# A causal retention layer with a gated unit behind it: the second double chunk's queries in a gate bank, its scores ahead of the first's values, the w_out load between two casts, and three double chunks with load buffers of their own

## The chip, the cores and the metric

The kernel runs on one NeuronCore of a Trainium2 chip. Its metric is the time on the device of one execution, in microseconds (us), as the median of repeated runs. TensorE is called PE here (PEld is its loading of weights), VectorE DVE, ScalarE ACT, GpSimd POOL, and SyncE, which issues most of the transfers, SP.

## The reference

Eight sequences of 576 tokens, 8 heads of 64 values each. The first half is retention: attention without a softmax, whose scores are causal and fall off with the distance by a factor gamma per head. The second is a gated unit: the retention's output, with the heads side by side (512 values per token), goes through a causal convolution of 5 taps per column and a sigmoid to make a gate, and through a matrix to make the value; the product goes through a second matrix.

```python
scores = scale * np.matmul(q, k.transpose(0, 1, 3, 2))      # per batch and head
gamma = 1.0 - 2.0 ** (-5.0 - np.arange(H))
Dmat = np.where(rel >= 0, gamma ** rel, 0.0)                # rel = query's place - key's place
x = np.matmul(scores * Dmat, v)                             # heads side by side: (B, S, 512)
for k in range(5):
    gate_pre += conv_w[k] * xp[:, k:k + S, :]               # xp: x with 4 zero rows ahead
gate = 1.0 / (1.0 + np.exp(-gate_pre))
out = (gate * (x @ w_val)) @ w_out
```

Inputs and output are float32; the kernel multiplies in bf16.

## The kernel before

The work is cut into 18 "double chunks", numbered from 0 in the list `dcs`. A sequence gives two full double chunks of 256 tokens; the last 64 tokens of four sequences together make a tail. The order is sequences 0 to 3 with two double chunks each, their tail (number 8), then sequences 4 to 7 and their tail (17). So double chunks 0 and 1 are the two of sequence 0, 2 and 3 those of sequence 1.

Gamma to the power of the distance is split into two factors: values are multiplied by `gin` when they are cast to bf16, and the result by `gout`. So a mask of zeros and ones is all that the scores need, and what earlier double chunks contribute is a state, keys times values, that is carried on.

For a double chunk m these are the steps, with the helper that issues each:

- `load` (through `fetch`, L87) issues three transfers of 512 KB on SP: keys, queries, values, into tiles `fk`, `fq`, `fv` of the pool `ld`. Double chunks 0 and 1 use tiles of the names `fke`, `fqe`, `fve`; all others share two buffers of each of `fk`, `fq`, `fv`, so the load of m+2 waits for the cast of m.
- `cast_k`, `cast_q` (L224) and `cast_v` (L240) turn them into bf16 on POOL: about 1.04, 1.04 and 1.90 us.
- `turn(0, m)` and `turn(1, m)` (L262) transpose keys and queries, 8 TensorE transposes each, into a PSUM bank: by default the only bank of the pool `ps_t` (`tps`), or one that is given. `take_turned` (L270) copies the bank into the tile `kq`, by default on ScalarE (1.02 us).
- `scores(m, r)` are 16 matmuls (L252, s<-kq) for each of the two halves r of the keys, into the banks s0 and s1 of `ps_s`. `masks` (L293) multiplies each bank by the mask on VectorE (0.69 us) into the tiles p0 and p1 of the pool `pp`, which has two buffers of each.
- `values` (L307, o<-p,vb) are 16 matmuls per r; `carried` (L307, o<-kq,sd) adds the state's part. `take_x` (L342) multiplies the two result banks by `gout` on VectorE into the long tile `x`. `pass_on` (L355) copies the last four columns of `x` to the next double chunk's tile on POOL; the convolution needs them.
- `update` (L252, st<-vb,kb) adds to the state, `take_state` (L377) copies it to bf16 on ScalarE.
- `conv` (L252, g<-x,dg) is the convolution as 40 matmuls with diagonal matrices; `gate` (L406) the sigmoid on ScalarE; `value` (L413) the matmuls with w_val in bf16 (`wvb`) and a product with the gate on VectorE (L416, tile z); `project` (L423) the matmuls with w_out (`wob`), a copy on ScalarE (L431) and the store. All of these use the pool `ps_g`, two PSUM banks of the name g: the gate banks.

The order on each engine is the program's: the body is written under a manual schedule, so engines run their instructions in the order of the text, and only waits between engines are added.

A prologue (L451 to L500) does double chunk 0 without its convolution, together with the constants. Dummy matmuls on a tile of zeros (`keep_warm`, L448) fill TensorE's waits. Then a loop runs m from 1 to 18. Pass m does the scores, values and state of double chunk m, and the convolution and gate of m-1; the values with w_val and the projections follow behind (in passes 2 and 3 those of the first two double chunks catch up). Pass m also turns keys and queries of m+1, casts m+2 and issues the loads of m+4.

Weights: w_val comes in three transfers, two on SP behind the loads of double chunk 2 (L109, L110) and one on ACT (L113). It is cast in two halves, `prep_wv(g_copy, 1)` on POOL at the end of the prologue and `prep_wv(s_copy, 0)` on ScalarE in pass 2 (L215). w_out comes in three transfers that POOL issues (L124, L126), which convert it to bf16 on the way.

Of the kernel before, what the change touches and what calls it, by code (L numbers as in the profile page):

```python
# [13 lines left out]
F32 = mybir.dt.float32  # L14
BF16 = mybir.dt.bfloat16
# [6 lines left out]
def kernel(  # L22
# [57 lines left out]
    with tc.manual_schedule():  # L80
# [12 lines left out]
                                      in_=src[GB * b + 2 * r + ab, :, c * W:S, :].rearrange("h p d -> p h d"))  # L93

        def load(name, m):
            t = ld.tile([P, H, R, D], F32, name=f"f{name}" + ("e" if m < 2 else ""))
            fetch(nc.sync, t, {"q": q, "k": k, "v": v}[name], m)
            loaded[name, m] = t

# [12 lines left out]
        def load_wv_rest():  # L112
            nc.scalar.dma_start(out=wv_dst[1, half[1]], in_=wv_src[1, 0])  # L113

        for name in "kqv":
            load(name, 3)


        ORDER = ((0, 0, 0, 1), (HP, 0, 1, 0), (0, 2, 0, 0), (HP, 2, 1, 1))
# [109 lines left out]
        def cast_k(m, *copies):  # L229
            cast("k", m, copies)  # L230

        def cast_q(m, *copies):
            cast("q", m, copies)
# [22 lines left out]
        def turn(which, m, bank=None):  # L256

            src = (kbf, qbf)[which][m]
            dst = new_bank() if bank is None else bank
            for pr in range(NP):  # L260
                for r in range(R):
                    nc.tensor.transpose(dst[:, pr, r, :], src[:, pr, r, :, :].rearrange("p i d -> p (i d)"), ident)  # L262
            return dst

        def take_turned(which, m, bank, *copies):
            if m not in kq:
                kq[m] = tp_sb.tile([P, 2, NP, R, P], BF16, name="kq", bufs=2)
            o = 0
            for (copy, n) in copies or ((nc.scalar.copy, NP),):
                copy(kq[m][:, which, o:o + n], bank[:, o:o + n])  # L270
                o += n
            assert o == NP
# [65 lines left out]
        def take_x(m, ab):  # L338
            kind, b, c = dcs[m]
            if kind == "full":  # L340
                t0, x0 = c * W + ab * P, PAD + ab * P
                nc.vector.tensor_tensor(  # L342
                    xg[b // GB][c][:, b % GB, :, x0:x0 + P].rearrange("p o (n r) -> p o r n", r=R),
                    ops[m, ab], gout[:, :, t0:t0 + P].rearrange("p o (r n) -> p o r n", r=R), op=ALU.mult)
            else:
                nc.vector.tensor_tensor(
                    xg[b][c][:, ab::2, :, PAD:].rearrange("p b o n -> p o b n"),
                    ops[m, ab], gout[:, :, c * W:S].unsqueeze(2).to_broadcast([P, NP, R, TAIL]), op=ALU.mult)

        def pass_on(m):  # L350

            kind, b, c = dcs[m]
            if kind == "full":
                x = xg[b // GB]
                nc.gpsimd.tensor_copy(x[c + 1][:, b % GB, :, 0:PAD], x[c][:, b % GB, :, W:W + PAD])  # L355
# [87 lines left out]
        def keep_warm(n, t=None):  # L443

            if t is None:
                t = ps_o.tile([P, NP, R, HP], F32, name="o0").rearrange("p o r n -> p (o r n)")
            for _ in range(n):
                nc.tensor.matmul(t, zeros[:, 0:P], zeros, start=True, stop=True)  # L448
# [28 lines left out]
        run(update(0, 0))  # L477
        take_state(0, 0)
        load_wv_rest()
        keep_warm(1)  # L480
        run(update(0, 1))
        take_state(0, 1)
        run(carried(0, 1))
        bank = turn(0, 1)
        take_turned(0, 1, bank)
        keep_warm(2, spare(ps_g, "g"))
        bank = turn(1, 1)
        take_turned(1, 1, bank)
        run(*values(0, 1))
        run(*values(0, 0))  # L490
        run(carried(0, 0))
        take_x(0, 0)
        take_x(0, 1)
        pass_on(0)
        keep_warm(4, spare(ps_g, "g"))
        for (name, f) in (("k", cast_k), ("q", cast_q), ("v", cast_v)):
            f(2)
            load(name, LB + 2)
        prep_wv(g_copy, 1)
        load_wo()  # L500

# [1 line left out]
        for m in range(1, ND + 1):  # L505
            now, nxt, last = ok(m), ok(m + 1), m == ND
            late = m < 4
            hi, lo = conv(m - 1)

            if now:  # L510
                run(scores(m, 0))
                masks(m, 0, 0)
                masks(m, 0, 1)
            if last:
                run(lo, hi)
                gate(m - 1, 1)
                gate(m - 1, 0)
            elif late:
                run(lo[0:8], hi[0:8])
                run(pairs(update(m, 0)), hi[8:10])  # L520
                take_state(m, 0)
                gate(m - 1, 0)
                run(pairs(update(m, 1)), lo[8:10])
                take_state(m, 1)
                gate(m - 1, 1)
                run(carried(m, 1))
            else:
                run(carried(m, 1))
                run(pairs(update(m, 1)), lo[0:2])
                take_state(m, 1)  # L530
                run(lo[2:10], hi[0:8])
                gate(m - 1, 1)
                run(pairs(update(m + 1, 0)), hi[8:10])
                take_state(m + 1, 0)
                gate(m - 1, 0)
            if now:
                run(scores(m, 1))
                masks(m, 1, 0)
                masks(m, 1, 1)

            if last:
                value(m - 1, 1, spare(ps_s, "s1"))
                value(m - 1, 0, spare(ps_s, "s0"))
                project(m - 2, 0)
                project(m - 2, 1)
                project(m - 1, 0, last=True)
                project(m - 1, 1, last=True)
                continue
            if nxt:
                bank = turn(0, m + 1)  # L550
                take_turned(0, m + 1, bank)

            if m == 2:
                prep_wv(s_copy, 0)
            for (f, n, i) in {1: (), 2: ((value, 0, 1), (value, 0, 0)),
                              3: ((value, 2, 1), (project, 0, 0), (project, 0, 1))}.get(
                                  m, ((value, m - 1, 1), (project, m - 2, 0))):
                f(n, i)
            if ok(m + 2):
                cast_k(m + 2)  # L560
                cast_q(m + 2)
                cast_v(m + 2)

            run(*values(m, 1))
            run(*values(m, 0))
            run(carried(m, 0))
            take_x(m, 0)
            take_x(m, 1)
            pass_on(m)

            if nxt:
                bank = turn(1, m + 1)
                take_turned(1, m + 1, bank)
            for (f, n, i) in {1: (), 2: ((value, 1, 1), (value, 1, 0)),
                              3: ((value, 2, 0), (project, 1, 0), (project, 1, 1))}.get(
                                  m, ((value, m - 1, 0), (project, m - 2, 1))):
                f(n, i)
            for name in "kqv":
                if ok(m + 2 + LB):
                    load(name, m + 2 + LB)  # L580
            if m == 3:
                run(update(m + 1, 0))
                take_state(m + 1, 0)
# [28 lines left out]
```

## Time and profile before

| | |
|---|---|
| median of 13 runs | 168.21 us (165.92 to 172.5) |
| the profiled execution | 168.04 us |
| its span in the profile | 166.2 us |
| around the span | 1.84 us |
| busy: PE, PEld, DVE, ACT, POOL | 88%, 65%, 60%, 55%, 48% of the span |
| moved by DMA | 39.82 MB, 240 GB/s over the span |
| start of pass 3 on TensorE | 35.52 us |

The span runs from the first to the last instruction that the hardware profiler saw. A line of a timeline gives the start, the length, the engine, the source line, the operation, output and input tiles, and in brackets the time that the engine stood idle just before and what ended it. "issue" there means that nothing which the profile shows was waited for. The clock is the share of TensorE's full clock that was granted.

### The profile page before, as it was taken

How to read it: one execution, taken by the hardware profiler on the slowest of the kernel's cores; microseconds unless marked ns; L12 is line 12 of the kernel's file. 1: busy time of each engine (PE TensorE's matmuls, PEld its weight loads, DVE VectorE, ACT ScalarE, POOL GpSimd, SP SyncE). 2: the span in 40 equal slices, each digit the busy share in tenths (PEclk: the TensorE clock that was granted, in tenths of full speed). 3: DMA queues.
4: the chain of work that ended last, by engine and by line, in shares of the span. 5: the costliest groups of instructions: out<-in, count | busy, mean ns of one | idle time of the engine just before them, and what ended most of it. 6: DMA issues, size and time to landing. Idle time of an engine off the chain costs nothing.

```text
span 166.2 us, 7603 instructions
## 1 busy us (share of the span) xinstructions
PE 146.4 (88%) x3350; PEld 107.2 (65%) x3383; DVE 100.4 (60%) x187; ACT 91.8 (55%) x149; POOL 80.0 (48%) x88
## 2 busy tenths in 40 slices
PE   6887638898999999999999997999699999999970
PEld 2455527575676867777677866686568778765620
DVE  6775461495447667666577765776567668666210
ACT  4774624426666657664667656575557575652340
POOL 4796569714883633457745734463727224000000
PEclk9999985799999999999999999999999999999997
DMA  4999999977999977999999698959994874131134
GB/s 141 345 347 309 310 265 241 273 171 197 293 373 310 302 174 182 289 332 324 347 335 296 226 297 234 325 184 311 307 312 133 190 180 181 37 130 65 66 126 126
DMA packets 70814, 39.82 MB, mean 240 GB/s; under 512 B 15978, under 2 KB 65662, under 8 KB 70782
## 3 DMA queue, kind: packets, MB, share of 16 engines
q1 hardware_dynamic: 68096, 38.28, 77.8%
q0 software_dynamic: 2352, 0.53, 2.6%
q10 hardware_dynamic: 334, 0.53, 1.2%
q8 instruction: 26, 0.43, 1.0%
q14 instruction: 6, 0.05, 0.1%
HBM read 30.42 MB, written 9.44 MB: 240 GB/s over the span
## 4 chain that ended last, share of the span: by engine, by line
PE 68%; DMA 15%; SPq 7%; issue 4%; ACT 2%; POOL 2%; DVE 1%; ACTq 0%
PE g L423 17%; PE g L413 15%; PE g L252 11%; DMA wob<-in_moe_w_out_dram 9%; PE tps L262 9%; PE o L307 7%; SPq L87 7%; DMA wvf<-in_moe_w_val_dram 6%; PE s L252 5%; PE st L252 2%; PE s L413 1%; ACT ob L431 1%; POOL wvb L215 1%; POOL wob L124 1%; DVE ob L429 1%
## 5 line engine op out<-in xcount | busy, mean ns | idle before, releaser
L293 DVE TENSOR_TENSOR p<-s,mask 128x512 bf16<-128x512 f32 x62 | 40.0, 686 | 23.1 <-PE s L252 23.0
L270 ACT COPY kq<-tps 128x1024 bf16<-128x1024 bf16 x34 | 34.6, 1018 | 17.1 <-PE tps L262 16.9
L240 POOL TENSOR_TENSOR vb<-fv,gin 128x1024 bf16<-128x1024 f32 x16 | 30.5, 1904 | 18.0 <-DMA fv<-in_v_dram 18.0
L413 PE MATMUL g<-x,wvb 128*128 128x256 bf16 x272 | 36.0, 277 | 0.8 <-ACT wvb L215 0.5
L423 PE MATMUL g<-wob,z 128*128 128x512 bf16 x113 | 34.8, 379 | 1.8
L252 PE MATMUL g<-x,dg 64*64 64x256 bf16 x720 | 32.1, 278 | 2.2 <-issue 1.4
L431 ACT COPY ob<-g 128x512 f32<-128x512 f32 x34 | 19.9, 586 | 24.7 <-PE g L423 21.8
L342 DVE TENSOR_TENSOR x<-o,gout 128x512 bf16<-128x512 f32 x32 | 22.2, 744 | 13.9 <-PE o L307 13.9
L416 DVE TENSOR_TENSOR z<-gate,g 128x512 bf16<-128x512 f32 x34 | 23.4, 687 | 10.7 <-PE g L413 9.9
L413 PEld LDWEIGHTS <-wvb 128*128 128x128 bf16 x288 | 27.0, 99 | 4.3 <-ACT wvb L215 1.0
L406 ACT ACTIVATE gate<-g 128x512 f32<-128x512 f32 x36 | 21.3, 604 | 10.7 <-PE g L252 5.4
L252 PEld LDWEIGHTS <-dg 64*64 64x64 bf16 x720 | 23.5, 107 | 5.5 <-issue 4.4
L224 POOL CAST qb<-fq 128x1024 bf16<-128x1024 f32 x16 | 16.7, 1043 | 9.6 <-PE tps L262 4.4
L423 PEld LDWEIGHTS <-z 128*128 128x128 bf16 x144 | 14.0, 98 | 10.8 <-issue 0.6
L224 POOL CAST kb<-fk 128x1024 bf16<-128x1024 f32 x16 | 16.7, 1044 | 5.4 <-DMA fk<-in_k_dram 5.1
L252 PE MATMUL s<-kq 64*64 64x128 bf16 (+1 forms) x560 | 16.3, 220 | 2.4 <-ACT kq L270 1.3
L252 PEld LDWEIGHTS <-kq 64*64 64x64 bf16 x576 | 11.8, 108 | 9.4 <-issue 8.8
L355 POOL COPY x<-x 128x16 bf16<-128x16 bf16 x16 | 3.2, 198 | 28.2 <-DVE x L342 28.2
L252 PE MATMUL st<-vb,kb 64*64 64x64 bf16 x512 | 14.1, 196 | 1.8 <-ACT sd L377 1.2
L377 ACT CAST sd<-st 128x256 bf16<-128x256 f32 x24 | 8.9, 370 | 11.8 <-PE g L252 7.1
L252 PEld LDWEIGHTS <-kb 64*64 64x64 bf16 x512 | 12.5, 112 | 3.4 <-issue 3.2
L262 PE MATMUL tps<-ident,kb 128*128 128x128 bf16 x144 | 12.0, 230 | 2.1 <-issue 1.5
(73 smaller groups left out, 120.8 us busy)
## 6 DMA issues: line engine op xcount, KB each, us to landing
out_dram<-ob SPq DMA_DIRECT2D x32, 256.0 KB, 3.9
fk<-in_k_dram SPq DMA_DIRECT2D x14, 512.0 KB, 5.9
fq<-in_q_dram SPq DMA_DIRECT2D x14, 512.0 KB, 6.4
fv<-in_v_dram SPq DMA_DIRECT2D x14, 512.0 KB, 7.5
fke<-in_k_dram SPq DMA_DIRECT2D x2, 512.0 KB, 5.0
fqe<-in_q_dram SPq DMA_DIRECT2D x2, 512.0 KB, 5.5
fve<-in_v_dram SPq DMA_DIRECT2D x2, 512.0 KB, 6.0
fk<-in_k_dram SPq DMA_DIRECT2D x8, 128.0 KB, 3.1
```

The lines of the kernel that those rows point to most:

```text
L224: copy(t[:, o:o + n], src[:, o:o + n])
L240: eng.tensor_tensor(vbf[m][:, h:h + n], loaded["v", m][:, h:h + n], g[:, h:h + n].unsqueeze(3).to_broadcast([P, n, R, D]), op=ALU.mult)
L252: return lambda: nc.tensor.matmul(*a, skip_group_check=True, **kw)
L262: nc.tensor.transpose(dst[:, pr, r, :], src[:, pr, r, :, :].rearrange("p i d -> p (i d)"), ident)
L270: copy(kq[m][:, which, o:o + n], bank[:, o:o + n])
L293: nc.vector.tensor_tensor(p[:, :, 0:n], sps[m, r][i][:, :, 0:n], mask[dcs[m][0], r].unsqueeze(1).to_broadcast([P, NP, n]), op=ALU.mult)
L342: nc.vector.tensor_tensor(xg[b // GB][c][:, b % GB, :, x0:x0 + P].rearrange("p o (n r) -> p o r n", r=R), ops[m, ab], gout[:, :, t0:t0 + P ...
L406: nc.scalar.activation(t, gps[n][i], AF.Sigmoid)
L413: nc.tensor.matmul(vps[:, j, :], lhsT=wvb[:, o, 2 * i + j, :], rhs=xs(n, slice(0, P), o, PAD), start=(j == 0 and o == 0), stop=(j == 1 and ...
L416: nc.vector.tensor_tensor(z, gsb[n][i], vps, op=ALU.mult)
L423: nc.tensor.matmul(o, lhsT=zsb[n, j // 2][:, j % 2, i * P:(i + 1) * P], rhs=wob[:, j, :], start=(j == 0), stop=(j == NP - 1))
L431: nc.scalar.copy(ob, o)
```

## The change

Six things are different.

- Double chunk 2 also gets load buffers of its own (three buffers of `fke`, `fqe`, `fve`), so the shared ones begin with double chunk 3, and the loads of double chunk 4 are issued at the start of the program behind those of 3 instead of between the casts of 2.
- In the prologue the queries of double chunk 1 are turned into a gate bank instead of `tps`, and copied half by ScalarE, half by VectorE.
- The first scores of double chunk 1 move from pass 1 into the prologue, ahead of the values of double chunk 0. Of their two masks one stands ahead of the x products of double chunk 0, one behind them.
- Keys of double chunk 2 are turned in the prologue (they were turned in pass 1), and its queries in pass 1 where the keys were, ahead of the values instead of behind them.
- In pass 2 the keys of double chunk 3 are turned behind the values of double chunk 0 with w_val instead of ahead of them.
- POOL casts keys and queries of double chunk 2 before it hands on x of double chunk 0, then issues the loads of w_out, then casts the values of double chunk 2 and its half of w_val. The dummy matmuls are placed differently; there are seven of them from there on as before.

```diff
@@ load
-            t = ld.tile([P, H, R, D], F32, name=f"f{name}" + ("e" if m < 2 else ""))
+            t = ld.tile([P, H, R, D], F32, name=f"f{name}" + ("e" if m < 3 else ""),
+                        bufs=3 if m < 3 else LB)
...
-        for name in "kqv":
-            load(name, 3)
+        for m in range(3, 5):
+            for name in "kqv":
+                load(name, m)
@@ prologue
         load_wv_rest()
-        keep_warm(1)
         run(update(0, 1))
         take_state(0, 1)
         run(carried(0, 1))
         bank = turn(0, 1)
         take_turned(0, 1, bank)
-        keep_warm(2, spare(ps_g, "g"))
-        bank = turn(1, 1)
-        take_turned(1, 1, bank)
+        bank = turn(1, 1, spare(ps_g, "g", [P, NP, R, P], BF16))
+        take_turned(1, 1, bank, (s_copy, 2), (v_copy, 2))
+        keep_warm(4)
+        run(scores(1, 0))
+        masks(1, 0, 0)
         run(*values(0, 1))
         run(*values(0, 0))
         run(carried(0, 0))
         take_x(0, 0)
         take_x(0, 1)
+        masks(1, 0, 1)
+        cast_k(2)
+        bank = turn(0, 2)
+        take_turned(0, 2, bank)
+        cast_q(2)
         pass_on(0)
-        keep_warm(4, spare(ps_g, "g"))
-        for (name, f) in (("k", cast_k), ("q", cast_q), ("v", cast_v)):
-            f(2)
-            load(name, LB + 2)
+        load_wo()
+        cast_v(2)
         prep_wv(g_copy, 1)
-        load_wo()
+        keep_warm(3, spare(ps_g, "g"))
@@ loop
-            if now:
+            if now and m > 1:
                 run(scores(m, 0))
                 masks(m, 0, 0)
                 masks(m, 0, 1)
...
-            if nxt:
-                bank = turn(0, m + 1)
-                take_turned(0, m + 1, bank)
+            def turn_keys():
+                if nxt and m > 1:
+                    bank = turn(0, m + 1)
+                    take_turned(0, m + 1, bank)
+
+            def turn_queries():
+                if nxt:
+                    bank = turn(1, m + 1)
+                    take_turned(1, m + 1, bank)
+
+            if m > 2:
+                turn_keys()
+            if m == 1:
+                turn_queries()
 
             if m == 2:
                 prep_wv(s_copy, 0)
...
                 f(n, i)
+            if m == 2:
+                turn_keys()
...
             pass_on(m)
 
-            if nxt:
-                bank = turn(1, m + 1)
-                take_turned(1, m + 1, bank)
+            if m > 1:
+                turn_queries()
```

## The prediction

> **What bounds the kernel now.** I read the page's busy shares and its 40 slices first, then TensorE's timeline up to 45 us, its busy time in stretches of 3.41 us, and last the timelines of POOL and SP. Below, "chunk" is a double chunk, counted from 0.
>
> ```profile
> PE 146.4 (88%) x3350; PEld 107.2 (65%) x3383; DVE 100.4 (60%) x187; ACT 91.8 (55%) x149; POOL 80.0 (48%) x88
> PE   6887638898999999999999997999699999999970
> ...
> PEclk9999985799999999999999999999999999999997
> ```
>
> TensorE is the bound, with eights and nines from slice 9 on (37 us). What is not full lies in the first 33 us: idle slices, and three at 8, 5 and 7 tenths of the clock. So the start decides: whatever makes the loop reach chunk 3 earlier comes off the end, if transfers keep up.
>
> ```profile
> 13.19 0.61 PE L262 MATMUL tps<-ident,qb 128*128 128x128 bf16 x8 [0.67 <-ACT kq L270]
> ...
> 15.84 1.07 PE L252 MATMUL g<-x,dg 64*64 64x256 bf16 x32
> ...
> 22.68 0.42 PE L252 MATMUL s<-kq 64*64 64x128 bf16 x16 [1.10 <-ACT kq L270]
> 22.90 0.42 PE L252 MATMUL g<-x,dg 64*64 64x256 bf16 x8
> 24.71 1.50 PE L252 MATMUL g<-x,dg 64*64 64x256 bf16 x24 [1.40 <-issue]
> ...
> 31.56 1.05 PE L413 MATMUL g<-x,wvb 128*128 128x256 bf16 x8 [0.52 <-ACT wvb L215]
> ...
> 35.52 0.42 PE L252 MATMUL s<-kq 64*64 64x128 bf16 x16
> ```
>
> This is TensorE's timeline (start, length, last the idle time and its releaser). 15.84 and 22.90 are the gate convolutions of chunks 0 and 1, 35.52 is the first instruction of chunk 3 (loop pass m=3): my milestone. Query turns wait because keys and queries share one bank (0.67, and behind it 1.10). The 1.40 us has no releaser. Counting TensorE's instructions in program order (weight loads too), it stands at about the 705th, the 0.30 us "issue" wait at 17.42 some 256 earlier, and those at 81.70, 101.62 and 117.75 again whole multiples of 256 on, give or take ten: the sign of instructions fetched in blocks.
>
> ```profile
> 17.20:20.61 3.41, 2.19 (x82) 1.75 (x86) 1.29 (x2) 2.76 (x5) 1.69 (x2) 1.00 1.12 305
> 20.61:24.03 3.42, 1.60 (x62) 1.17 (x50) 2.28 (x4) 1.01 (x1) 1.96 (x3) 1.00 0.96 260
> 24.03:27.44 3.41, 2.29 (x63) 1.96 (x65) 0.39 (x1) 0.77 (x2) 3.41 (x5) 0.50 1.02 276
> 27.44:30.86 3.42, 3.42 (x51) 2.61 (x43) 1.29 (x2) 2.37 (x5) 3.42 (x5) 0.50 1.13 240
> ```
>
> Columns: stretch, length, busy PE, PEld, DVE, ACT, POOL (with counts), clock, DMA share, GB/s. After a stretch with TensorE 47% busy the clock is halved for 6.8 us; after 64% it was not.
>
> **The change, part by part.**
>
> *Chunk 1's queries in a gate bank, its scores early.* The query turn no longer waits for the key copy: its cast ends at 11.01+1.04 = 12.05. ScalarE copies the keys at 12.12–13.13, then its half of the queries (0.585, the 128x512 row) to 13.72; VectorE's half waits for that (as its row at 8.70 does) and adds 0.42: 14.17, against 14.84 before. But four dummy matmuls and the scores now stand ahead of chunk 0's values, which move from 13.72 to 14.4. One mask (0.65) stands ahead of the two x products on VectorE. It also waits for the r=1 values: the mask tiles have two buffers each, both full. So the mask runs 14.9–15.55, the x products (1.37) until 16.92 instead of 15.78, and the convolution starts at 16.98: **+1.14 us**. Behind the waiting mask stand just those x products, and the convolution waits for them.
>
> *Chunk 2's keys ahead of the loop, its queries in their place, no turn at the end of m=1.* The 8 transposes lie where TensorE waits for x anyway (15.4–16.0; the key cast, freed of waiting for the hand-over of x, runs 14.35–15.4). Before, convolution to end of scores took 15.84–18.82; if the block at 17.42 is now in time (it is wanted 0.84 later and came 0.30 late), scores end at 19.66. Masks 19.75–21.05, values 21.1, x at 21.86–23.23 (21.03–22.40 before). Query copy 20.3–21.3, so the 1.10 us wait goes: scores of chunk 2 at 21.8. What is late next is x: convolution of chunk 1 at 23.25, **+0.35** on 22.90.
>
> *The block and the clock.* Not to be seen in advance. If the block is there, 20.61–24.03 holds values and state products 0.75, scores 0.4, convolution 0.78: 1.93 of 3.42, 56%, between the 47% that halved the clock and the 64% that didn't. If it comes as late as before, 46%. A wait for it costs between 0 and (7.29 us from one crossing to the arrival, 17.42 to 24.71, laid on the new crossing at 18.26) 25.55−23.65 = 1.9 us. Most blocks of the steady part are run through in about 5 us without a wait, and this one would be asked for 5.3 us later; I take 0 and full clock.
>
> [...]
>
> *Chunk 3's keys behind the values of chunk 0 in m=2.* From 23.25, convolution and state updates take 2.63−0.30 = 2.33 (m=1's own rows), scores to 25.93, value 1 to 26.8. ScalarE now casts its half of w_val straight after the gates (26.55–27.7, rows 1.14) instead of behind a 1.01 us key copy; value 0 waits for it, 27.7–28.6. Key turn to 29.05, values and state products to 29.75, key copy 29.25–30.26, so the query turn waits 0.5 (one bank again), 30.3–30.75; two values (1.84 before) and m=3 starts at 32.6: **−2.9** on 35.52.
>
> *w_out earlier.* Its issue (0.92+1.63) moves on POOL from behind w_val's cast to behind the hand-over of x, about 17.1–19.7, ahead of chunk 2's value cast, which waits for its transfer till 19.73 anyway, and ahead of w_val's cast, which started at 23.09 when its last piece landed. So it costs POOL nothing, and chunk 3's key cast moves from 26.70 to 24.25. If that cover goes, values of chunk 2 are late by up to 2.5 us, of which 4.3 are spare (21.63 to their use at 25.99). Gain: the projections at 40.12 stood 0.4 us for w_out (8 matmuls in 2.11 against 8 x 0.216): **−0.4**. [...]
>
> *Own buffers.* SP issued without a break from 18.57 to 24 us, so chunk 4's loads were not waiting for buffers: nothing.
>
> *Give-back.* Chunk 5's v cast ended at 46.29 and is used at 48.39; 3.3 us earlier means 45.09. If transfers land as before, **+1.2**; if they follow the earlier casts, 0. I take 1.2.
>
> **Sum**: 168.04 (span 166.2 and 1.84 around it) − 2.9 − 0.4 + 1.2 = **165.9 us**. The profiled execution is 0.17 below the median of 168.21.
>
> **Rivals.**
>
> *Block late and half clock again (0.34).* For: the 46% above. From a restart at 24.71 to 25.55 half-clock rows give scores ending 28.35, value 1 until 30.1, value 0 until 31.0, key turn, then a query turn at 32.65 and m=3 at 34.95, each plus up to 0.84: −0.6 to +0.3, with w_out's −0.4 167.0 to 167.9. Here the parts cancel: what the bank saves goes to the later x.
>
> *w_out in the way (0.20): slower.* Its transfer now flies beside w_val and chunk 3's loads.
>
> ```profile
> 24.20 0.92 POOL L124 DMA_DIRECT2D wob<-in_moe_w_out_dram  x1
> ...
> 26.70 1.08 POOL L224 CAST kb<-fk 128x1024 bf16<-128x1024 f32 x1
> ...
> 39.58 1.90 POOL L240 TENSOR_TENSOR vb<-fv,gin 128x1024 bf16<-128x1024 f32 x1 [5.79 <-DMA fv<-in_v_dram]
> ```
>
> While it flew (24.2 to 41.0), a v transfer took 13.8 us to land, against a median of 7.5: 6.3 more. On chunk 3's keys (landed by 26.70) that means 33.0, cast 34.04, and from key turn to m=3 it is 4.0: 38.05, +2.5, less 0.4: 170.1. It decides from a landing after 30.9 on. Against: the neighbours of w_out before had slack, and 4.2 us must be lost first. [...]
>
> *The rest (0.02)*: the clock lost for more stretches, above 171.
>
> **Chances.** One per cent (1.7 us) is about what a measurement of this kernel can tell. Forecast 0.44 (164.7 with no give-back to 166.3), all faster; late block 0.34, same; w_out 0.20 and the rest 0.02, slower. Range: 164.3 (no give-back and half of the 0.9 us that chunk 2's value 0 waits) to 170.1. The forecast's own range is 164.3–166.3.
>
> **What would show it.** Right: convolution of chunk 0 about 17.0 and of chunk 1 about 23.3, without an issue wait behind its first matmuls; clock 1.0 over 24–31; m=3 near 32.6; w_out landed before the first projection; a wait for chunk 5's values near 45. Wrong: half clock again, a key cast of chunk 3 beginning after 31, or x of chunk 0 well after 17.

## The result, and the profile after

| | before | after |
|---|---|---|
| median, with the number of runs | 168.03 us (48 runs, 165.92 to 172.5) | 168.09 us (11 runs, 164.22 to 169.13) |
| mean of all these runs | 168.37 ± 0.22 us | 167.36 ± 0.49 us |
| ratio | | 0.990, 95% interval 0.985 to 0.995 |
| the profiled execution, its span | 168.04, 166.2 us | 168.8, 167.1 us |

The ratio leaves out the runs that are over 1.5% above the fastest of their kernel (in the result that leaves 4 of the changed kernel's 11), so it can say "1.0% faster" although the two plain medians agree. Because the single runs are spread over 5 to 7 us, I give the mean of all runs (± its standard error) beside every ratio below. The changed kernel was timed twice more in the experiments. The means of all three sets put it below the kernel before, by 0.9 to 1.6 us; the ratios of the two repeats are 1.0000 and 0.9986, and by themselves they show no difference. So the direction rests on the means and on the traces, and the size is less certain than the first interval suggests.

The profiled execution of the changed kernel is not its median: its span is 0.9 us longer than the one of before. What that 0.9 us is made of can be read off, and it is the main lesson of this case. First the page of the changed kernel (busy shares, TensorE's 40 slices and the granted clock in tenths; its line numbers are two higher than before).

```profile
PE 146.1 (87%) x3349; PEld 107.1 (64%) x3383; DVE 100.7 (60%) x188; ACT 91.3 (55%) x149; POOL 80.2 (48%) x88
...
PE   6888746898999999999979979999799999999970
...
PEclk9999996999999999999999999999999999999999
```

The hole in the clock is shorter (one slice at 6 tenths where there were 8, 5 and 7), and the slices before it are filled no better. TensorE's timeline (start, length, the instruction, the idle time before it and what ended it):

```profile
14.56 0.31 PE L254 MATMUL s<-kq 64*64 64x128 bf16 x8 [0.28 <-ACT kq L272]
...
17.62 1.07 PE L254 MATMUL g<-x,dg 64*64 64x256 bf16 x32 [0.53 <-DVE x L344]
...
19.03 0.30 PE L254 MATMUL g<-x,dg 64*64 64x256 bf16 x2 [0.22 <-issue]
...
22.57 0.43 PE L254 MATMUL s<-kq 64*64 64x128 bf16 x16
24.22 0.41 PE L254 MATMUL g<-x,dg 64*64 64x256 bf16 x8 [1.21 <-DVE x L344]
26.05 1.08 PE L254 MATMUL g<-x,dg 64*64 64x256 bf16 x24 [1.43 <-issue]
...
33.28 0.61 PE L264 MATMUL tps<-ident,qb 128*128 128x128 bf16 x8 [0.42 <-ACT kq L272]
...
35.57 0.42 PE L254 MATMUL s<-kq 64*64 64x128 bf16 x16
```

The 0.67 and 1.10 us waits for the key copy are gone. In their place stand 0.53 and 1.21 us for x, as the prediction said. But the wait without a releaser is back behind the same eight matmuls, and just as long: 1.43 us at 26.05 (1.40 at 24.71 before). Pass 3 starts at 35.57, not at 32.6. The stretches that held the clock show what follows from the wait (busy PE, PEld, DVE, ACT, POOL, then clock, DMA share, GB/s):

```profile
20.61:24.03 3.42, 1.78 (x67) 1.43 (x64) 2.53 (x4) 1.61 (x3) 2.81 (x4) 1.00 1.19 304
24.03:27.44 3.41, 1.80 (x52) 1.45 (x53) 1.30 (x3) 0.00 (x0) 0.97 (x1) 0.87 1.24 228
27.44:30.86 3.42, 2.92 (x57) 2.09 (x50) 1.42 (x3) 2.77 (x6) 1.04 (x1) 0.63 0.78 185
```

TensorE is 52% and 53% busy in the first two, and the clock is halved towards the end of the second. In the profiles here the half clock lasts 3.4 (result), 6.8 (before) or 10.2 us (e1), that is one, two or three steps of 3.41 us, and the stretches above are not in line with these steps. The following ones are, in the same columns: two of this profile, then one of the first repeat of the changed kernel (e0) and one of a run with dummy matmuls (f1), both described below.

```profile
23.13:26.54 3.41, 0.90 (x28) 0.63 (x32) 2.20 (x4) 0.00 (x0) 1.87 (x3) 1.00 1.27 214
26.54:29.95 3.41, 2.98 (x80) 2.40 (x69) 0.59 (x1) 2.08 (x5) 1.04 (x1) 0.50 0.87 211
...
20.05:23.46 3.41, 1.86 (x75) 1.46 (x64) 2.43 (x4) 1.70 (x3) 3.08 (x4) 1.00 1.17 311
...
23.38:26.79 3.41, 1.79 (x48) 1.12 (x47) 1.84 (x4) 0.00 (x0) 1.44 (x2) 1.00 1.24 219
```

Here the clock fell after a step in which TensorE was 26% busy, and for one step; in the kernel before it was halved for two. In the first repeat it fell after one of 55%, for two steps; in f1 it stayed full after one of 52%. POOL's timeline answers the questions on w_out:

```profile
17.77 0.92 POOL L126 DMA_DIRECT2D wob<-in_moe_w_out_dram  x1
18.68 1.63 POOL L128 DMA_DIRECT2D wob<-in_moe_w_out_dram  x2
...
23.97 1.03 POOL L226 CAST kb<-fk 128x1024 bf16<-128x1024 f32 x1
...
32.77 1.90 POOL L242 TENSOR_TENSOR vb<-fv,gin 128x1024 bf16<-128x1024 f32 x1 [4.15 <-DMA fv<-in_v_dram]
...
41.98 1.90 POOL L242 TENSOR_TENSOR vb<-fv,gin 128x1024 bf16<-128x1024 f32 x1 [0.46 <-DMA fv<-in_v_dram]
```

The issue is where it was put, and chunk 3's keys are cast at 23.97 without a wait (in the second repeat at 25.30, behind 1.50 us for their transfer). Its values come 4 us later than before (32.77 against 28.68), and chunk 5's are cast by 43.88, earlier than before (46.29). w_out itself has left the chain of waits, where its transfer made up 9% before.

**Stage by stage in four profiles.** Chunk 0's first scores come at 8.6 to 9.0 us in some executions of the changed kernel and its variants and at 9.6 to 9.7 in others, so I count from them. (The kernel before has one profile as it is, 8.72, and one with dummies, 9.03.) The two rows marked "again" are the changed kernel as it is, profiled in two of the runs below.

| | first scores | convolution of chunk 0, behind them | of chunk 1 | start of pass 3 | state update of chunk 4 | late issue waits | span |
|---|---|---|---|---|---|---|---|
| before | 8.72 | 7.12 | 14.18 | 26.80 | 37.42 | 2.76 | 166.2 |
| predicted | 8.72 | 8.26 | 14.53 | 23.88 | | | |
| after | 9.62 | 8.00 | 14.60 | 25.95 | 36.43 | 3.58 | 167.1 |
| after, again (first) | 9.71 | 7.90 | 14.03 | 25.27 | 35.74 | 2.98 | 165.7 |
| after, again (second) | 8.73 | 8.03 | 14.63 | 25.95 | 36.43 | 3.52 | 166.0 |

"Late issue waits" are the waits of TensorE that end on "issue" behind 40 us, added up. From the state update to the end, less these, it is 117.30 us before and 117.47, 117.27 and 117.32 after: nothing else changes there. So the span of the profiled execution is 166.2 + 0.90 (first scores) − 0.85 (to pass 3) − 0.14 (to the state update) + 0.82 (late waits) + 0.17 = 167.1. The change is the two terms in the middle: −1.0 us, −1.7 and −1.0 in the three profiles. The outer two differ between executions of the changed kernel by as much; of the kernel before there is only this profile.

The first repeat is not like the other two: the block wait in front of the rest of chunk 1's convolution was 0.26 us there, against 1.43 and 1.42, but the clock was halved for 6.8 us instead of 3.4.

### The profile page after: what moved, and what is told of

Same layout as the page of the kernel before. It is cut to its first block, busy times and chain, and to the rows that moved or that the text cites. A ratio compares the mean times of both kernels' runs of the same rounds, so it can differ in the third digit from the quotient of the medians.

```text
span 167.1 us, 7600 instructions
## 1 busy us (share of the span) xinstructions
PE 146.1 (87%) x3349; PEld 107.1 (64%) x3383; DVE 100.7 (60%) x188; ACT 91.3 (55%) x149; POOL 80.2 (48%) x88
## 4 chain that ended last, share of the span: by engine, by line
PE 77%; issue 6%; ACT 5%; DVE 4%; DMA 3%; POOL 2%; SPq 1%; ACTq 0%; DVEq 0%; POOLq 0%
PE g L415 18%; PE g L425 17%; PE g L254 14%; PE tps L264 10%; PE o L309 8%; PE s L254 5%; PE st L254 4%; DMA fve<-in_v_dram 3%; POOL vb L242 1%; ACT kq L272 1%; DVE x L344 1%; DVE p L295 1%; PE s L415 1%; ACT sd L379 1%; ACT gate L408 1%
## 5 line engine op out<-in xcount | busy, mean ns | idle before, releaser
L272 ACT COPY kq<-tps 128x1024 bf16<-128x1024 bf16 x33 | 33.6, 1018 | 17.3 <-PE tps L264 17.1
L242 POOL TENSOR_TENSOR vb<-fv,gin 128x1024 bf16<-128x1024 f32 x15 | 28.5, 1903 | 15.2 <-DMA fv<-in_v_dram 15.2
L415 PE MATMUL g<-x,wvb 128*128 128x256 bf16 x272 | 35.4, 274 | 0.3 <-ACT gate L408 0.2
L254 PE MATMUL g<-x,dg 64*64 64x256 bf16 x720 | 31.5, 275 | 4.1 <-DVE x L344 1.7
L254 PEld LDWEIGHTS <-dg 64*64 64x64 bf16 x720 | 23.0, 106 | 7.6 <-issue 5.3
L226 POOL CAST qb<-fq 128x1024 bf16<-128x1024 f32 x15 | 15.6, 1040 | 10.3 <-PE g L254 3.1
L226 POOL CAST kb<-fk 128x1024 bf16<-128x1024 f32 x15 | 15.6, 1040 | 3.1 <-DMA fk<-in_k_dram 1.6
L379 ACT CAST sd<-st 128x256 bf16<-128x256 f32 x24 | 8.9, 370 | 12.2 <-PE g L254 10.3
L309 PEld LDWEIGHTS <-vb 64*64 64x64 bf16 x576 | 8.6, 107 | 7.3 <-issue 7.1
```

Of the source, the lines that this page charges most:

```text
L226: copy(t[:, o:o + n], src[:, o:o + n])
L242: eng.tensor_tensor(vbf[m][:, h:h + n], loaded["v", m][:, h:h + n], g[:, h:h + n].unsqueeze(3).to_broadcast([P, n, R, D]), op=ALU.mult)
L254: return lambda: nc.tensor.matmul(*a, skip_group_check=True, **kw)
L309: nc.tensor.matmul(o, start=key not in opened, stop=False, skip_group_check=True, **kw)
L415: nc.tensor.matmul(vps[:, j, :], lhsT=wvb[:, o, 2 * i + j, :], rhs=xs(n, slice(0, P), o, PAD), start=(j == 0 and o == 0), stop=(j == 1 and ...
```

## The experiments

First all their times. "Difference" is the mean of all runs less that of the kernel before, timed beside it; the ratio, too, is to the kernel before.

| run | median, us | ratio (95%) | difference, us |
|---|---|---|---|
| e0_changed | 167.08 | 1.0000 (0.9944 to 1.0056) | −1.6 ± 0.6 |
| e1_mask_behind_x | 168.62 | 0.9932 (0.9827 to 1.0036) | −1.0 ± 0.6 |
| e2_shift28 (6 runs) | 166.96 | 0.9882 (0.9716 to 1.0047) | −2.3 ± 1.1 |
| e3_wout_behind | 167.85 | 1.0012 (0.9939 to 1.0085) | −1.2 ± 0.7 |
| f1_dummies | 167.38 | 0.9963 (0.9907 to 1.0020) | −1.4 ± 0.5 |
| f2_late_loads | 169.32 | 0.9886 (0.9793 to 0.9979) | +0.2 ± 0.6 |
| f3_keys_ahead | 167.92 | 0.9973 (0.9910 to 1.0035) | −0.4 ± 0.6 |
| f4_before_dummies | 168.08 | 0.9945 (0.9887 to 1.0002) | −0.6 ± 0.5 |
| h0_changed_again | 167.58 | 0.9986 (0.9937 to 1.0036) | −0.9 ± 0.4 |
| h1_shift_and_dummies | 168.14 | 0.9986 (0.9945 to 1.0027) | −0.1 ± 0.5 |
| h2_scores_in_the_loop | 167.66 | 0.9991 (0.9946 to 1.0036) | −0.6 ± 0.5 |
| h3_chunk4_held_back | 167.79 | 0.9949 (0.9904 to 0.9995) | −0.6 ± 0.4 |

Differences of half a us are below what these times can tell. What the experiments tell apart they tell in the timelines.

### The changed kernel again

> The changed kernel itself, beside the variants. Theory F (instruction blocks): TensorE's wait without a releaser again stands behind the first 8 matmuls of chunk 1's convolution and ends 6 to 7.5 us after the block before it was entered; where the clock then falls the pass m=3 starts about 35.5 us, where it doesn't about 34. Theory W (w_out in the way): chunk 3's v transfer lands after 31 us and something on TensorE waits for it; by F nothing does, since the values are first used after 37. Time 0.98 to 1.00 of the kernel before by F, above 1.00 by W.

> The changed kernel once more, as the partner of the other three runs of this call. From the runs so far (mean of all 23 of its times 167.36, of 77 of the kernel before about 168.6) its time should be 0.5 to 1.7 us below the kernel before, with an interval that may still touch 1.0, and its profile should again have an issue wait of 0.6 to 1.5 us behind the first matmuls of chunk 1's convolution.

Ratios of 1.0000 and 0.9986, differences of −1.6 ± 0.6 and −0.9 ± 0.4 us. With the −1.0 ± 0.5 of the result they make −1.1 ± 0.3 us, weighted by their errors. The result's 0.990 is at the favourable end. The waits on issue of the second one, all from TensorE's timeline:

```profile
18.17 0.30 PE L254 MATMUL g<-x,dg 64*64 64x256 bf16 x2 [0.22 <-issue]
...
25.19 1.06 PE L254 MATMUL g<-x,dg 64*64 64x256 bf16 x24 [1.42 <-issue]
...
55.42 0.38 PE L254 MATMUL g<-x,dg 64*64 64x256 bf16 x5 [0.46 <-issue]
...
81.53 0.31 PE L309 MATMUL o<-kq,sl 64*64 64x64 bf16 x14 [0.34 <-issue]
...
102.07 0.30 PE L254 MATMUL s<-kq 64*64 64x128 bf16 x7 [0.95 <-issue]
...
119.02 0.62 PE L264 MATMUL tps<-ident,kb 128*128 128x128 bf16 x8 [1.77 <-issue]
```

The same program waited at 87.06 (1.18 us), 99.27 (1.15) and 120.17 (1.25) in the profile of the result. So the late waits vary by themselves. The one at 25.19 is the one that matters here: it ends 7.02 us after the one at 18.17 ended, and in the result's profile 26.05 − 19.03 is 7.02 too.

### Is it a block of instructions?

Two of the warming-up matmuls of the prologue are replaced by 16 small ones of 64x64, also on zeros. With the weight load of each, all of TensorE's instructions behind come 28 places later in its program; the work stays.

```diff
-        keep_warm(3)
+        keep_warm(1)
+        small(16)
```

> Three dummy matmuls of the start become one and 16 small ones, so all later TensorE instructions stand 28 places further on; no work is changed. Theory F: the wait without a releaser moves back by 28 instructions, from behind 8 matmuls of chunk 1's convolution into the scores of chunk 2 ahead of it (behind about 10 of the 16), and the later waits of the steady part stand 28 places earlier too. Rival (the wait belongs to the convolution: its operands, its bank or the convolution's shape): it stays behind the first 8 matmuls of the convolution. Time within 0.5% of the changed kernel either way.

TensorE's timeline of this run:

```profile
24.66 0.30 PE L254 MATMUL s<-kq 64*64 64x128 bf16 x6 [2.63 <-issue]
24.74 1.27 PE L254 MATMUL g<-x,dg 64*64 64x256 bf16 x32
```

The wait left the convolution and stands behind the tenth of chunk 2's scores, where the count had put it, and it is longer because TensorE gets there earlier (at 22.03 us, against 23.77 in the second repeat). So the wait keeps its place in the count of instructions, whatever instruction stands there. The pages of before and after also list a DMA queue of the kind "instruction", with 26 packets and 0.43 MB in each. One of these packets passes at 22.37 to 23.36 us before and at 23.74 to 24.69 after, and the wait ends 1.35 and 1.36 us behind it (24.71 and 26.05). From these places and times I read it as a wait for the program itself. The late waits summed to 0.16 us in this profile, and its span was the shortest of all, 162.1. To see whether that belongs to the shift, the shift was run once more together with seven dummy matmuls:

> The changed kernel with both additions at once: TensorE's instructions moved on by 28 (one small matmul more for each instruction that the shorter warming-up leaves out, as in the run with 16 small dummies) and the 3 + 4 dummies of the run that kept the clock. Theory A (late fetch of an instruction block in the head plus half clock are what is left to win): the block wait still stands early in chunk 2's scores or just behind them, 1 to 2.7 us, the clock stays at 0.9 or more up to 35 us, and pass 3 starts at about 34.2; the late waits depend on where the 256-instruction crossings fall, and with 7 more instructions behind the shift they are at most 0.5 us if the shift removes them, 2 to 3.5 us if they vary by themselves. Time 164.0 to 166.0 if the shift removes late waits; 167.0 to 168.0 if they vary by themselves from execution to execution.

The late waits were 2.56 us, and the time was that of the kernel before (ratio 0.9986). The head wait was 3.36 us behind seven of the scores, the four dummies after it ran at the halved clock (1.89 us for the four, 1.04 in f1), and pass 3 began 30.1 us behind the first scores. So a shift moves the early wait and does not remove the late ones: my expectation that the clock stays up and pass 3 comes at 34 fell. That the shift is an improvement is not shown: e2's six runs leave it open, and h1 shows none.

### The clock by itself

The same dummies, three ahead of chunk 1's values and four ahead of its convolution, in the changed kernel, and seven in the kernel before:

```diff
+            if m == 2:
+                keep_warm(4, spare(ps_t, "tps"))
...
             if m == 1:
                 turn_queries()
+                keep_warm(3, spare(ps_g, "g"))
```

> The changed kernel with seven more dummy matmuls where TensorE stands still: three in pass 1 ahead of the values of chunk 1, four in pass 2 ahead of the convolution of chunk 1. Theory K (the clock): the half-clock time in the head comes from too little work there; with 1.5 us more of it the mean granted clock of the runs rises from 0.981 to above 0.988 and the mean time falls by 1 to 1.5 us. Theory F (instruction blocks) expects the wait without a releaser 14 instructions earlier, behind the first matmuls of the convolution, and if that wait alone drops the clock the mean clock stays within 0.003 of the changed kernel's and the time within 0.5 us.

> The kernel before, with seven dummy matmuls in its two gaps of pass 1 (three ahead of the values of chunk 1, four while the query copy is waited for). Theory K: its mean clock rises from 0.9825 to above 0.988 and its mean time falls by 1 to 1.5 us, so that it equals the changed kernel. If the clock is lost in the wait for the instruction block instead, clock and time stay within 0.003 and 0.5 us.

The clock on the page of the changed kernel with dummies:

```profile
PEclk9999999999999999999999999999999999999997
```

And the place of the wait on its TensorE timeline:

```profile
25.77 1.07 PE L254 MATMUL g<-x,dg 64*64 64x256 bf16 x31 [1.37 <-issue]
```

The clock stays full, and the wait stays at 1.37 us, behind one matmul in place of eight, as seven dummies with their weight loads must have it. Pass 3 begins 25.2 us behind the first scores, 0.1 to 0.8 earlier than without them, and the wait does not go away with the half clock. In the kernel before, pass 3 comes at 25.4 instead of 26.8 with the dummies, at a wait of 1.27; its time falls by 0.6 ± 0.5. The mean clock rose to 0.991 and 0.992, as Theory K said, but neither time fell by the 1 to 1.5 us it had for that.

What the half clock costs is read from the end of the block wait to pass 3: 9.1 us in f1 and 9.2 in e3 (both at full clock), 9.5 in the two profiles of the changed kernel with 3.4 us of half clock, 10.3 in the one with 6.8; in the kernel before 9.9 with the dummies and 10.8 without. That is about half a us for 3.4 us of half clock and about one for 6.8, as estimates: the waits of the stage are not the same in all of them. Set beside each other at full clock, f4 and f1, one profile each, the change is worth 0.2 us at pass 3 (25.40 and 25.19).

### Do the transfers hold the block up?

The loads of chunks 3 and 4 are held back until POOL has cast its half of w_val: a memset of one column of each tile, placed there, makes them wait. Then the same for chunk 4 alone.

```diff
+            if 3 <= m < 5:
+                nc.gpsimd.memset(t[:, 0, 0, 0:1], 0.0)
...
         prep_wv(g_copy, 1)
+        for m in range(3, 5):
+            for name in "kqv":
+                load(name, m)
```

> The changed kernel with the loads of chunks 3 and 4 held back behind POOL's cast of w_val (about 24 us), so that from some 18 to 24 us only w_val's rest and w_out are moved. Theory F with transfers as its cause: the block for the convolution of chunk 1 arrives in under 5.5 us, and the wait without a releaser (0.3 to 1.4 us so far) is gone; pass 3 is then late for another reason, since its keys land after 28 us. If blocks take 7 us whatever else is moved, the wait stays at 0.3 us or more. The whole is slower by 1 to 4 us either way.

> The changed kernel with only chunk 4's three loads held back until POOL has cast w_val's piece (about 23 us); chunk 3's loads go out at once. Theory A (the block of instructions is late because of the transfers that are in flight beside it): the issue wait behind chunk 1's first convolution matmuls falls from 1.0-1.4 us to 0.5 or less, the clock stays nearer to full, pass 3 starts at about 33.5 to 34.5 since chunk 3's keys and queries land as early as before or earlier, and chunk 4's keys, landing by about 36, still come in time; time 0.5 to 1.5 us below the changed kernel. Theory B (the block takes its 7 us whatever flies): the wait stays above 0.8 us and the time is within 0.5 us of the changed kernel.

With both held back, TensorE's timeline has no wait on issue in the head at all (its line numbers are two lower):

```profile
22.96 1.07 PE L252 MATMUL g<-x,dg 64*64 64x256 bf16 x32 [1.22 <-DVE x L342]
...
25.46 1.05 PE L413 MATMUL g<-x,wvb 128*128 128x256 bf16 x8
...
33.36 1.03 PE L262 MATMUL tps<-ident,kb 128*128 128x128 bf16 x8 [5.09 <-POOL kb L224]
```

From the convolution of chunk 1 to the first value it is 2.50 us, against 5.0 after (23.36 to 28.36 in the second repeat) and 2.68 predicted: without the wait, TensorE goes as I had drawn it. But chunk 3's keys, loaded late, then stop it for 5.09 us, and pass 3 starts at 39.7. (Its median and its mean are not below those of before, although its ratio is 0.989.) What was in flight: from 17.2 to 24.0 us the 16 DMA engines were busy to 0.76 and 0.87 here, to 1.12 and 1.20 in the second repeat of the changed kernel. With chunk 4 alone held back they were still at 1.11 and 1.19, and the block came as late as ever:

```profile
19.32 0.30 PE L255 MATMUL g<-x,dg 64*64 64x256 bf16 x2 [0.52 <-issue]
...
26.07 1.11 PE L255 MATMUL g<-x,dg 64*64 64x256 bf16 x24 [1.14 <-issue]
```

That is 6.75 us from one to the other. Its time is that of the changed kernel within half a us. So holding back both sets of loads freed the block, in the one profile taken, and holding back chunk 4's alone did not; chunk 3's alone was not tried. The share of busy DMA engines by itself does not explain it. Later in the kernel 256 instructions pass in less time beside transfers just as dense, without a wait (second repeat, from one multiple of 256 to the next):

```profile
81.54:85.92 4.38, 4.38 (x128) 3.43 (x131) 3.27 (x5) 2.06 (x4) 2.34 (x3) 1.00 1.10 340
```

What makes the block late beside the early transfers stays open. A placement that frees the block and still brings chunk 3 in time was not found.

### The single steps

The first mask moved behind the x products (e1), and the scores and masks of chunk 1 put back into pass 1, with their queries still in the gate bank (h2):

```diff
         run(scores(1, 0))
-        masks(1, 0, 0)
...
         take_x(0, 1)
+        masks(1, 0, 0)
```

> Only the first mask of chunk 1 moves behind the two x products of chunk 0; everything else as in the changed kernel. If the later x is the cost of the early scores, as the prediction has it, the convolution of chunk 0 starts 0.6 to 0.7 us earlier after the first scores than in the changed kernel (8.0 us there, so 7.3), the block of instructions is entered earlier by the same and the whole is 0.5 to 0.8 us faster (ratio to the changed kernel 0.995 to 0.997). Rival: the block's arrival is fixed by the transfers around it and not by the entry into the block before; then the convolution waits longer and nothing is gained.

> The changed kernel with chunk 1's scores and masks back at the head of pass 1, behind the convolution of chunk 0, while its queries still go to the gate bank. Theory A (my first step: the mask in front of the x products makes the convolution of chunk 0 0.8 to 1.1 us later, and the early scores give that back before pass 3, so the step is worth nothing by itself): convolution of chunk 0 at 7.1 to 7.3 us after the first scores instead of 7.9 to 8.0, start of pass 3 as in the changed kernel within 0.5 us, time within 0.5 us of it. Theory B (having scores early is where the gain comes from): pass 3 starts 0.8 us or more later than in the changed kernel of the same call, time up by as much.

The convolution of chunk 0 came 7.81 and 8.06 us behind the first scores, against 7.90 to 8.03 after. I had expected the whole delay to go. It does not, and these lines of the second run, from TensorE's timeline, say why (the scores of chunk 1 stand ahead of the convolution there, as in the kernel before):

```profile
15.48 0.62 PE L264 MATMUL tps<-ident,kb 128*128 128x128 bf16 x8 [1.08 <-POOL kb L226]
15.94 0.81 PE L450 MATMUL g<-zeros 128*128 128x512 bf16 x3
16.68 0.42 PE L254 MATMUL s<-kq 64*64 64x128 bf16 x16
16.92 1.05 PE L254 MATMUL g<-x,dg 64*64 64x256 bf16 x32
```

The key turn of chunk 2 now stands in front of the convolution, and it waits for POOL's cast of these keys, until 15.4. x was ready at 15.7 in that run, 1.2 us ahead of the convolution. Two limits lie on top of each other: the mask in front of x, and the key cast in front of the turn. Both runs take away the first and leave the second; the second was not taken away alone. In e1 the block at the crossing before then came 0.68 us late, the clock was halved for 10.2 us and pass 3 came 27.54 us behind the first scores, so nothing was gained there, as its rival had it. The early scores themselves gave 0.25 us at pass 3 (26.20 against 25.95 in the second repeat of the changed kernel, timed beside it and with the same 1.42 us wait for the block): that is within half a us, as expected of a step that pays for itself and no more.

The key turn of chunk 3 put back ahead of the values in pass 2 (f3), and w_out issued behind w_val's cast again (e3):

```diff
-            if m > 2:
+            if m > 1:
                 turn_keys()
...
-            if m == 2:
-                turn_keys()
```

> The changed kernel with the keys of chunk 3 turned ahead of the values in pass 2, as before. By the prediction's fifth step ScalarE then casts its half of w_val behind a 1.01 us key copy again and TensorE waits for it: from the second scores of chunk 2 to pass 3 it takes 7.8 to 8.2 us as in the kernel before (8.03), against 7.16 in the changed kernel; mean time 0.5 to 1 us above the changed kernel's. Rival: the query turn's wait for its bank gives all of it back the other way, and the two are within 0.3 us.

```diff
-        load_wo()
         cast_v(2)
         prep_wv(g_copy, 1)
+        load_wo()
```

> The changed kernel with the loads of w_out issued behind the casts of chunk 2's values and of w_val, as before. Theory F: chunk 3's v transfer lands 2 to 4 us earlier, the first projections wait for w_out again by about 0.4 us, and the time is the changed kernel's plus 0 to 0.5 us. Theory W: w_out beside chunk 3's loads cost time, so this variant is faster than the changed kernel by 1 us or more, and the waits on TensorE before 30 us get shorter.

With the keys ahead, the convolution of chunk 1 to pass 3 takes 11.79 us, against 11.24, 11.35 and 11.32 after: the step gives about 0.5 us, at a clock that is halved in all of them. With w_out behind, pass 3 to the state update of chunk 4 takes 10.65 us against 10.47 and 10.48 (10.62 before): the earlier issue gives 0.14 to 0.18 us from there on. A wait for it is to be seen in the projections of that run:

```profile
39.01 0.38 PE L425 MATMUL g<-wob,z 128*128 128x512 bf16 x1
39.55 1.24 PE L425 MATMUL g<-wob,z 128*128 128x512 bf16 x5 [0.16 <-DMA wob<-in_moe_w_out_dram]
```

The block wait was 0.64 us there, the clock stayed full, and pass 3 came 24.27 us behind the first scores, 1.0 to 1.7 earlier than in the three profiles of the changed kernel. Whether w_out's later place did that, or this execution, is open: the block came 6.2 us after the crossing before it (found by counting instructions), against 6.1 and 7.0 in profiles with w_out early, and the time shows no gain. That chunk 2 has load buffers of its own was not undone alone.

## Why the prediction was right, and where it was not

Forecast: 165.9 us, 2.3 below the median of before shown with it. Measured: faster, by a ratio of 0.990 (−1.7 us) in the result and by −1.1 ± 0.3 us over all runs. The range held, and so did the direction, as far as the means and the traces can tell it. The size is about half, and the sum holds one wrong step and one that partly made up for it. I use the second repeat of the changed kernel, whose first scores are at 8.73 us, as in the profile that the prediction was worked from.

1. *Chunk 1's queries in a gate bank.* Convolution of chunk 0 at 16.76, predicted 16.98: +0.92 for +1.14. In the result's profile the mask is released by the r=1 values, as predicted; on VectorE's timeline:

```profile
15.60 0.69 DVE L295 TENSOR_TENSOR p<-s,mask 128x512 bf16<-128x512 f32 x1 [0.63 <-PE o L309]
16.21 1.36 DVE L344 TENSOR_TENSOR x<-o,gout 128x512 bf16<-128x512 f32 x2
```

   What I missed is the second limit. I let the key turn lie "where TensorE waits for x anyway"; by e1 and h2 it is about as late as x by itself.
2. *Chunk 2's keys ahead of the loop.* Convolution of chunk 1 at 23.36, predicted 23.25. The 1.10 us wait went, and x was what came next. The crossing at 18.17, taken as in time, still cost 0.22 us.
3. *The block and the clock* is the step that failed. I took 0 and full clock from bounds of 0 to 1.9; it cost 1.42 us and a half clock again, for 3.4 us. The prediction held both halves of the right answer: 7.29 us from one crossing to the arrival, laid on the new crossing, gave 25.55, and it arrived at 25.19. I set that aside because most later blocks come without a wait. The one row that showed this block, in this place and under this load, was the 7.29. That the 256 instructions come as a block fits the runs: the wait moved with the count of instructions in e2, by the 28 places of the shift, and before and after it ended 1.35 and 1.36 us behind a packet of the instruction queue. In the six profiles in which the crossing before it has a wait of its own it ended 6.75 to 7.3 us after that; where the crossing has to be found by counting, it is 6.1 us (first repeat) to 7.5 (h1).
4. *Chunk 3's keys behind the values.* From the convolution of chunk 1 to pass 3 I predicted 9.35 us; it took 11.32 (12.62 before). The 1.97 us more are the block wait (1.42) and the half clock on updates and scores (0.9, from 2.74 against 2.33 and 0.84 against 0.35), less 0.3 for a shorter wait for w_val's cast. What I had counted as the gain of this step was mostly the wait and the half clock of before, which came back. Its own part is about 0.5 by f3. The 0.42 us wait of the query turn is the predicted 0.5.
5. *w_out earlier.* −0.14 for −0.4. I took the whole excess of eight matmuls for a wait; they take 1.97 us with w_out long there.
6. *Give-back.* Predicted +1.2, none came: pass 3 was not early enough, and chunk 5's values are cast by 44.95 us (43.88 in the result's profile), 1.3 earlier than before.

Sum, as measured: −0.84 (pass 3 at 34.68) − 0.14 = −1.0; predicted −2.9 − 0.4 + 1.2 = −2.1. The −0.84 can be taken apart, as an estimate from the times from the block's arrival to pass 3: the block came 0.48 us later than before, the steps behind it are worth −0.75 (f1 against f4, both at full clock), and the remaining −0.6 is that the half clock lasted 3.4 us and not 6.8. The last part was not forecast and looks like luck: the first repeat of the same program had 6.8 us of it, and a short block wait.

Of the rivals, *Block late and half clock again* is the one that the traces show in its mechanism (in the second repeat a block wait of 1.42 us and a half clock of 3.4 us). It put m=3 at 34.95 to 35.79, with the first scores at 8.72; seen was 34.68 with the first scores at 8.73, and counted from the first scores all three profiles are 0.3 to 1.0 us earlier than its range. Its time, 167.0 to 167.9, takes in the means of all three sets of runs, 167.36, 167.36 and 167.58. So by the traces this rival was the better forecast, and the forecast was right in sign for a smaller reason. *w_out in the way* did not happen: its point was chunk 3's keys landing after 30.9, and they were cast at 23.68 to 25.30 in the three profiles. A transfer did land late beside w_out, as that rival says, but it was chunk 3's values, 4 us later in the result's profile, and these are not used before 37 us there. That w_out in its new place makes the block or the clock worse is not excluded (e3).

On the clock: the 47% and 64% of the kernel before are not bounds of a rule. Taken in step with the clock, it fell after steps that were 26% busy (result), 27% (second repeat) and 55% (first repeat), and stayed full after one of 52% (f1), with no idle stretch of TensorE above 1.43 us in any of these. So my 56% could have gone either way; what the clock goes by, these runs do not show.

## What to carry to other kernels

Count instructions where a wait has no releaser. Here it stood a whole number of 256s from other such waits; moving TensorE's work about did not remove it (1.37 us in f1, 2.63 in e2, 3.36 in h1), and most of the time gained ahead of it was waited for there. Price it with the one row that shows the same place under the same load, and not with the quieter stretches later. When a step is freed from one limit, ask what else arrives at that moment: here a mask and a cast were both about 1 us late, and removing the mask gained 0.2 us at most.

When single runs spread over 5 to 7 us, take the profiled spans apart (start, stage by stage, sum of late waits) before comparing them: a change of 1 us can be read from its stage, even where the span of its profile is longer.

## What was not expected of the hardware

- The block of instructions for the convolution of chunk 1 came 6.1 to 7.5 us after the crossing before it in thirteen profiles, and in under 5.4 us, without a wait, in the one with the loads of chunks 3 and 4 held back (f2). The share of busy DMA engines alone does not tell the two apart: later blocks passed in 4.4 us at a share of 1.10.
- Late waits of this kind sum to between 0.16 and 4.8 us per execution over the fourteen profiles, in places that differ between executions of one program. In twelve of the fourteen, the time from chunk 4's state update to the end, less these waits, is 117.1 to 117.6 us; in the other two 118.3 (h3) and 118.9 (f3, whose clock was halved once more from 121.9 to 125.4 us). So they make most of what differs behind 46 us.
- The first scores of chunk 0 come at 8.6 to 9.0 us or at 9.6 to 9.7 us, in different executions of the same kernel (8.73, 9.62 and 9.71 in the changed one). In all six profiles with the late start the 8 transposes of chunk 0's queries take 1.06 us, in the other eight 0.61 to 0.62, for example in the result's profile and in the second repeat:

```profile
7.87 1.06 PE L264 MATMUL g<-ident,qb 128*128 128x128 bf16 x8
...
7.44 0.62 PE L264 MATMUL g<-ident,qb 128*128 128x128 bf16 x8 [0.41 <-POOL qb L226]
```

  The same 8 transposes of the kernel before take 1.03 us at 28.33, where the clock is 0.50, and 0.62 at 33.22, where it is 1.00. So the late start goes with what looks, by these lengths, like a half clock that lasts longer at the beginning; that is an estimate, since the clock column of the result's profile has 1.00 from 7 to 9 us. Whether the kernel before has it too, its two profiles cannot say.
